# Loads, masks and the order of weight conversion in the opening of a decay-attention and softplus-FFN kernel

## The chip, the cores and the metric

One core of a Trainium2 chip. The metric is the device time of the whole program in microseconds (us). The kernel before was run three times: 659.26 us in the median, 658.81 the lowest, 661.81 the highest. One more execution was profiled.

## The reference

Linear attention with a decay per head, then a feed-forward network (FFN) with softplus:

```python
gamma = 1.0 - 2.0 ** (-5.0 - np.arange(H, dtype=np.float32))       # B, H, S, D = 4, 8, 768, 64
for t in range(S):
    state = gamma[None, :, None, None] * state + np.einsum('bhd,bhe->bhde', k[:, :, t], v[:, :, t])
    y[:, :, t] = scale * np.einsum('bhd,bhde->bhe', q[:, :, t], state)
x = y.transpose(0, 2, 1, 3).reshape(B * S, H * D)                     # 3072 tokens of 512
h = x @ w_in                                                          # 512 x 2048
g = np.maximum(h, 0.0) + np.log1p(np.exp(-np.abs(h)))
out = g @ w_out                                                       # 2048 x 512
```

All inputs reach the kernel as in the reference, the two weights as 64-bit words.

## The kernel before

**Units.** Attention runs in 48 units: a chunk of 128 tokens of one batch, and one half of the heads (four heads). A unit has loads of q, k and v (128 KB each), a decay of q and v on GpSimd (`decay`), transposes of k and q on TensorE into one PSUM bank (`tp`) with copies into `kz` (one half on ScalarE, one on VectorE) and `qs` (`operands`), scores (`sc`, `scores_whole`), a copy of the scores to SBUF on ScalarE (L268) and the causal mask on GpSimd (`mask`, L260), an update of the state (`stp`), and the product (`yp`, `outputs`), whose result is split into a high and a low part, `xh` and `xl`. There is one `kz`, written anew by each unit. Units below `WHOLE` (12) work so; later ones load blocks of 32 tokens and transpose on VectorE.

**FFN.** Four units make a pair of chunks (256 tokens). Steps are (pairs, f): `hidden` multiplies by two blocks of 128 columns of w_in, `softplus` works on VectorE, ScalarE and GpSimd, and `second`, LAG (2) steps later, multiplies by the two blocks of w_out. Steps 0 to 3 (below `TURN`) are pair 0 with f 0 to 7, steps 4 to 11 pair 1 with f 0 to 15, and from step 12 on pair 0 (f 8 to 15) goes with pair 2, and so on. Every matmul of the FFN is made of three with split operands.

**Weights.** There are 16 blocks f of w_in and of w_out, 512 KB each in 64-bit words. A block is loaded by SP and converted: for w_in one operation of ScalarE (L85), three of VectorE (L93 to L95), a cast on ScalarE (L97) and the low half on GpSimd (L98); for w_out one of the VectorE operations is on ScalarE (L91). `load_weights(f)` issues w_in f and w_out f; from f = FETCH (3) on, each waits for the conversion of block f - FETCH of its kind. `convert_weights(f)` converts w_in f and then w_out f.

**Order.** The program is written in ticks (16 for a unit; `PARTS` says at which tick a part of a unit comes), with the weights put between them, and after each step `convert_to` sets how many blocks are converted by then. A planner that estimates times turns this into an order for each engine and for the SP queue; only from step 12 on is TensorE's order the written one. Two units are loaded ahead of everything, then w_in 0 and w_out 0, then units and weights in turn. `block_decays` (written at step 4) loads a small table, `qblocks`, with 16 DMAs (L538) and extends it on GpSimd (L544); unit 12 is the first to use it. `attention_bank` gives the PSUM bank of `tp`, `sc` and `yp`, by turns `acc3` and `a`.

Of the kernel before, what the change touches and what calls it, by code (L numbers as in the profile page):

```python
# [11 lines left out]
F32R = mybir.dt.float32r  # L12
I64 = mybir.dt.int64
# [4 lines left out]
P = 128  # L18
# [5 lines left out]
EARLY = 2  # L24
# [4 lines left out]
FETCH = 3  # L29
# [4 lines left out]
def decay_attention_then_softplus_ffn(ctx: ExitStack, tc: tile.TileContext, q, k, v, w_in, w_out, qtab, vtab, gtab, out):  # L34
# [25 lines left out]
    ident = const.tile([P, P], F32, name="ident")  # L60

# [3 lines left out]
    def load_weights(f):  # L65
        fs = slice(f * P, (f + 1) * P)
        raw[f] = [const.tile([P, ND * P], I64, name=nm, tag=f"{nm}{f}") for nm in ("win", "wout")]
        loads_of_f = (
            nc.sync.dma_start(raw[f][0].rearrange("p (c w) -> p c w", c=ND), w_in[:, fs].rearrange("(c p) w -> p c w", p=P)),
            nc.sync.dma_start(raw[f][1], w_out[fs, :]),  # L70
        )

        if f >= FETCH:
            for load, after in zip(loads_of_f, converts[f - FETCH]):
                tc.add_manual_dep(load.ins, after.name, mybir.DependencyInfo(mybir.DependencyClass.Sync, mybir.DependencyReason.SCHED_ONLY), reason="pace")

    def convert_weights(f):

        n = ND * P
        converts[f] = []  # L80
        for nm, bits, to in zip(("win", "wout"), raw.pop(f), (win, wout)):
            words = bits.bitcast(U32).rearrange("p (n t) -> p n t", t=2)
            low, high = words[:, :, 0], words[:, :, 1]

            nc.scalar.activation(high.bitcast(F32), high.bitcast(F32), AF.Copy, scale=2.0**-112)  # L85

            wp = ps_o.tile([P, n], U32, name="wp", tag="acc2")
            w = ffn.tile([P, n], U32, name="w", tag="o")

            if nm == "wout":  # L90
                nc.scalar.activation(wp, low, AF.Copy, scale=(1 - SLACK) * 2.0**-29, bias=7.5 * SLACK - 0.5)  # L91
            else:
                nc.vector.tensor_scalar(wp, low, 29, None, op0=ALU.logical_shift_right)  # L93
            nc.vector.scalar_tensor_tensor(wp, high, 0x80000000, wp, op0=ALU.bitwise_and, op1=ALU.bitwise_or)
            nc.vector.scalar_tensor_tensor(w, high, 3, wp, op0=ALU.logical_shift_left, op1=ALU.bitwise_or)  # L95
            to[f] = const.tile([P, 2, n], F32R, name=f"{nm}hl", tag=f"{nm}{f}")
            converts[f].append(nc.scalar.copy(to[f][:, 0], w.bitcast(F32)).ins)  # L97
            nc.gpsimd.tensor_tensor(to[f][:, 1], w.bitcast(F32), to[f][:, 0].bitcast(F32), op=ALU.subtract)  # L98

# [22 lines left out]
    vns = [attn.tile([P, HH, 2, D], F32, name=f"vn{i}") for i in range(3)]  # L122

# [32 lines left out]
    def tokens_of(n):  # L156
        t = vns[n % 3]
# [60 lines left out]
    def attention_bank(n, shape, name):  # L218
        taken.append(n)
        if n < WHOLE and len(taken) % 2:  # L220
            return ps_o.tile(shape, F32, name=name, tag="acc3")
        return ps_a.tile(shape, F32, name=name, tag="a")
# [108 lines left out]
    def outputs(n):  # L331
# [4 lines left out]
        if n < WHOLE:  # L336
            kn, vn, a = rest
            yp = attention_bank(n, [P, NJ, C], "yp")
            v0 = vns[n % 3].rearrange("p h t d -> p (h t) d")
# [57 lines left out]
    FIRST_TICK = -24  # L397
    PERIOD = 16
# [97 lines left out]

    def convert_to(n):
        nonlocal loaded, converted
        while converted < min(NF, n):
            convert_weights(converted)  # L500
            converted += 1
            if loaded < NF:
                load_weights(loaded)
                loaded += 1


    for n in range(2):
        load_unit(n)

# [36 lines left out]
    while done < ticks_for(0):  # L546
# [5 lines left out]
        if done % (4 * TICK) == 3 * TICK and done > 0 or done < 0 and loaded == 0:  # L552
            if loaded >= FETCH:
                convert_weights(converted)
                converted += 1
            load_weights(loaded)
            loaded += 1
# [92 lines left out]
```

## Time and profile before

| what | us |
|---|---|
| median of 3 runs | 659.26 |
| lowest and highest run | 658.81, 661.81 |
| profiled execution, its own time | 661.7 |
| its span, first to last instruction | 660.0 |
| TensorE (PE) busy | 648.3 |
| VectorE (DVE) busy | 411.9 |
| ScalarE (ACT) busy | 366.7 |
| GpSimd (POOL) busy | 319.3 |

The page gives busy times over the whole span, and matmuls overlap, so a busy TensorE is not yet one at its peak. The table of windows gives the same for stretches, with the granted clock of TensorE (1.00 is 2.4 GHz, 0.50 is 1.2 GHz) and the share of the DMA engines. The timeline shows single instructions, and in brackets how long an engine stood idle before one and what ended that. SP's rows are issues, not transfers. Names left of `<-` are written, those right of it read; L12 is line 12 of the kernel.

### The profile page before, as it was taken

Reading aid. Unit: us, or ns where it says so; the run is one execution under the profiler, and the core shown is the slowest. Engines: PE = TensorE matmul, PEld = TensorE weight load, DVE = VectorE, ACT = ScalarE, POOL = GpSimd, SP = SyncE. Lnnn points to the kernel's source line nnn. Section 1 sums busy time; section 2 is a strip of 40 time slices with the busy share of each in tenths; the row PEclk is TensorE's granted clock in tenths of the full one; section 3 lists DMA queues with packets and bytes.
Section 4 is the critical chain, followed back from the end, with each engine's and each line's share of the span. In section 5 each row is a group of like instructions: output and inputs, shape, how many; then the busy total and the mean of one; then the engine's idle time right before and its main releaser. Section 6 shows DMA issues by size and latency. Waiting matters only on the chain.

```text
span 660.0 us, 11777 instructions
## 1 busy us (share of the span) xinstructions
PE 648.3 (98%) x3762; PEld 555.2 (84%) x3762; DVE 411.9 (62%) x756; ACT 366.7 (56%) x799; POOL 319.3 (48%) x330
## 2 busy tenths in 40 slices
PE   7999999999999999999999999999999999999997
PEld 6898899888888888888888888888888888888896
DVE  5777888875685576576566665676677567522221
ACT  5867876656564555556565655565565555422221
POOL 5777758564445445444543464355345543332221
PEclk9999999999999999999999999999999999999999
DMA  9898573132223241131232132131222200000000
GB/s 241 227 260 239 161 195 86 37 76 41 42 62 62 39 96 21 26 84 35 40 84 37 35 92 35 17 82 29 46 61 48 41 19 33 0 1 33 0 33 32
DMA packets 153822, 46.69 MB, mean 71 GB/s; under 512 B 140448, under 2 KB 148640, under 8 KB 153760
## 3 DMA queue, kind: packets, MB, share of 16 engines
q1 hardware_dynamic: 153312, 45.93, 29.3%
q8 instruction: 29, 0.48, 0.3%
q14 instruction: 33, 0.27, 0.1%
q10 hardware_dynamic: 448, 0.01, 0.0%
HBM read 39.60 MB, written 6.29 MB: 70 GB/s over the span
## 4 chain that ended last, share of the span: by engine, by line
PE 92%; DMA 2%; ACT 2%; POOL 1%; issue 0%; DVE 0%; SPq 0%; POOLq 0%; ACTq 0%
PE hp L436 13%; PE hp L438 13%; PE acc L471 13%; PE acc L472 13%; PE hp L437 13%; PE acc L473 13%; PE yp L355 6%; PE sc L280 3%; PE stp L307 2%; DMA win<-in_moe_w_in_dram 2%; PE yp L345 1%; PE sc L267 1%; DMA vn<-in_v_dram 1%; PE yp L342 1%; PE tp L232 0%
## 5 line engine op out<-in xcount | busy, mean ns | idle before, releaser
L453 POOL TENSOR_TENSOR gl<-sp,gh 128x512 fp32r<-128x512 f32 x96 | 129.4, 1349 | 122.5 <-ACT gh L451 118.2
L436 PE MATMUL hp<-xh,winhl 128*128 128x512 f32 (+1 forms) x448 | 166.1, 371 | 1.0 <-DVE sp L449 0.5
L438 PE MATMUL hp<-xh,winhl 128*128 128x512 f32 (+1 forms) x448 | 162.0, 362 | 0.5 <-POOL winhl L98 0.5
L437 PE MATMUL hp<-xl,winhl 128*128 128x512 f32 (+1 forms) x448 | 161.7, 361 | 0.0
L445 ACT ACTIVATE sp<-sp 128x512 f32<-128x512 f32 x96 | 60.7, 632 | 167.7 <-DVE sp L444 167.6
L471 PE MATMUL acc<-wouthl,gh 128*128 128x512 f32 x384 | 151.0, 393 | 0.0
L472 PE MATMUL acc<-wouthl,gh 128*128 128x512 f32 x384 | 150.3, 391 | 0.0
L473 PE MATMUL acc<-wouthl,gl 128*128 128x512 f32 x384 | 149.0, 390 | 0.0
L444 DVE TENSOR_SCALAR sp<-hp 128x512 uint32<-128x512 uint32 x96 | 66.3, 690 | 84.8 <-PE hp L438 62.4
L438 PEld LDWEIGHTS hp<-xh,winhl 128*128 128x128 f32 x448 | 84.5, 189 | 14.3 <-POOL winhl L98 0.9
L436 PEld LDWEIGHTS hp<-xh,winhl 128*128 128x128 f32 x448 | 84.6, 189 | 12.3 <-PE yp L345 0.7
L437 PEld LDWEIGHTS hp<-xl,winhl 128*128 128x128 f32 x448 | 84.8, 189 | 11.2
L451 ACT CAST gh<-sp 128x512 fp32r<-128x512 f32 x96 | 59.7, 621 | 52.1 <-PE acc L472 40.0
L449 DVE SCALAR_TENSOR_TENSOR sp<-hp,sp 128x512 f32<-128x512 f32 x96 | 65.2, 680 | 33.7 <-ACT sp L445 33.2
L260 POOL TENSOR_SCALAR_AFFINE_SELECT a<-a 128x512 f32<-128x512 f32 x48 | 36.6, 762 | 101.6 <-DVE a L281 97.1
L473 PEld LDWEIGHTS acc<-wouthl,gl 128*128 128x128 f32 x384 | 71.8, 188 | 15.1
L471 PEld LDWEIGHTS acc<-wouthl,gh 128*128 128x128 f32 x384 | 72.1, 188 | 12.4
L472 PEld LDWEIGHTS acc<-wouthl,gh 128*128 128x128 f32 x384 | 72.4, 189 | 12.0
L213 POOL TENSOR_TENSOR vn<-vn,vtabs 128x256 f32<-128x256 f32 x48 | 29.8, 621 | 83.6 <-DMA vn<-in_v_dram 71.8
L281 DVE TENSOR_REDUCE a<-sc 128x256 f32<-128x512 f32 x72 | 49.3, 685 | 4.3 <-PE sc L280 3.5
L292 POOL TENSOR_TENSOR al<-a,ah 128x512 fp32r<-128x512 f32 x36 | 47.9, 1331 | 3.1 <-ACT ah L291 3.1
L329 DVE TENSOR_TENSOR st<-stp,st 64x128 fp32r<-64x128 f32 x60 | 17.3, 289 | 44.8 <-ACT st L327 44.2
(94 smaller groups left out, 919.3 us busy)
## 6 DMA issues: line engine op xcount, KB each, us to landing
win<-in_moe_w_in_dram SPq DMA_DIRECT2D x16, 512.0 KB, 4.9
wout<-in_moe_w_out_dram SPq DMA_DIRECT2D x16, 512.0 KB, 4.4
vn<-in_v_dram SPq DMA_DIRECT2D x48, 128.0 KB, 2.8
out_dram<-o SPq DMA_DIRECT2D x24, 256.0 KB, 2.1
vn<-in_k_dram SPq DMA_DIRECT2D x30, 128.0 KB, 2.4
kb<-in_k_dram SPq DMA_DIRECT2D x208, 16.0 KB, 1.7
qb<-in_q_dram SPq DMA_DIRECT2D x208, 16.0 KB, 1.7
qn<-in_q_dram SPq DMA_DIRECT2D x12, 128.0 KB, 4.9
```

Of the source, the lines that this page charges most:

```text
L281: summed[n] = nc.vector.tensor_reduce(sums[n][:, 2 * j:2 * j + 2, :], sc.rearrange("p h t c -> p h c t"), axis=mybir.AxisListType.X, op=AL ...
L436: nc.tensor.matmul(to, lhsT=wt[:, 0, d, :], rhs=xh[:, d], start=d == 0, stop=False)
L437: nc.tensor.matmul(to, lhsT=wt[:, 0, d, :], rhs=xl[:, d], start=False, stop=False)
L438: nc.tensor.matmul(to, lhsT=wt[:, 1, d, :], rhs=xh[:, d], start=False, stop=d == ND - 1)
L444: nc.vector.tensor_scalar(sp.bitcast(U32), hps[s].bitcast(U32), 0x80000000, None, op0=ALU.bitwise_or)
L445: nc.scalar.activation(sp, sp, AF.Softplus)
L449: nc.vector.scalar_tensor_tensor(g, hps.pop(s), 0.0, g, op0=ALU.max, op1=ALU.add)
L451: nc.scalar.copy(gh, g)
L453: nc.gpsimd.tensor_tensor(gl, sps.pop(s), gh.bitcast(F32), op=ALU.subtract)
L471: nc.tensor.matmul(to, lhsT=gh[:, k, ts], rhs=wt[:, 0], start=first, stop=False)
L472: nc.tensor.matmul(to, lhsT=gh[:, k, ts], rhs=wt[:, 1], start=False, stop=False)
L473: nc.tensor.matmul(to, lhsT=gl[:, k, ts], rhs=wt[:, 0], start=False, stop=last)
```

## The change

The loads of weights become a list of items, w_in 0, w_in 1, then w_in f and w_out f - 2 by turns, and w_out 14 and 15. Loads and conversions go by item, loads up to six items ahead of conversions. Units 0 to 3 are loaded ahead of all weights; unit 3's v has a tile of its own, in a buffer of `sp`. A table `INITIAL` says by which tick how many items are loaded and converted. For units 0 to 3 the mask is an AND with a table of all ones or zero bits on VectorE, which reads the scores from PSUM and writes them to SBUF. `qblocks` is copied out of `qtabs` on VectorE. The turns of the two PSUM banks are swapped.

```diff
-EARLY = 2
-FETCH = 3
+FETCH = 6
...
+    items = [("win", f) for f in range(2)] + [it for f in range(2, NF) for it in (("win", f), ("wout", f - 2))]
+    items += [("wout", f) for f in range(NF - 2, NF)]
+    def load_item(i):
+        nm, f = items[i]
...
+        if i >= FETCH:
+            paced_by(load, i - FETCH)
...
+    def convert_item(i):
...
+    vns.append(ffn.tile([P, HH, 2, D], F32, name="vn3", tag="sp"))
+    def v_tile(n):
+        return vns[3 if n == 3 else n % 3]
...
-        if n < WHOLE and len(taken) % 2:
+        if n < WHOLE and len(taken) % 2 == 0:
             return ps_o.tile(shape, F32, name=name, tag="acc3")
...
-        nc.scalar.copy(a, sc)
-        mask(a)
+        if n < 4:
+            keep = causal.bitcast(U32).unsqueeze(1).broadcast_to([P, HH, C])
+            nc.vector.tensor_tensor(a.bitcast(U32), sc.bitcast(U32), keep, op=ALU.bitwise_and)
+        else:
+            nc.scalar.copy(a, sc)
+            mask(a)
...
+    INITIAL = {12: (4, 0), 28: (6, 1), 44: (6, 2), 60: (6, 4), 76: (6, 5)}
...
+    def load_to(n):
+        while loaded < min(len(items), n):
+            load_item(loaded)
+            loaded += 1
...
+        while converted < min(len(items), n):
+            convert_item(converted)
             converted += 1
+            load_to(converted + FETCH)
...
-    for n in range(2):
+    for n in range(4):
         load_unit(n)
+    load_to(2)
...
+    keep = causal.bitcast(F32)
+    nc.gpsimd.memset(keep, -1.0)
+    nc.gpsimd.affine_select(keep, keep, pattern=[[1, C]], compare_op=ALU.is_ge, fill=0.0, base=0, channel_multiplier=-1)
+    nc.vector.tensor_copy(causal, keep)
...
-        for at in range(0, P, 32):
+        for par, half, _ in sides:
+            at = half.start
             for i in range(C // 32):
-                nc.sync.dma_start(
-                    qblocks[at:at + 32, 0, :, :, i].rearrange("p f m -> p (f m)"), qtab[i * 32:(i + 1) * 32, at // D:H:2]
+                nc.vector.tensor_copy(
+                    qblocks[at:at + 32, 0, :, :, i].rearrange("p f m -> p (f m)"), qtabs[i * 32:(i + 1) * 32, 0, par:H:2]
                 )
+            nc.vector.tensor_copy(qblocks[at + 32:at + 64, 0], qblocks[at:at + 32, 0])
...
-        if done % (4 * TICK) == 3 * TICK and done > 0 or done < 0 and loaded == 0:
-            if loaded >= FETCH:
-                convert_weights(converted)
-                converted += 1
-            load_weights(loaded)
-            loaded += 1
+        if done in INITIAL:
+            load_to(INITIAL[done][0])
+            convert_to(INITIAL[done][1])
...
-        convert_to(fs[-1] + 1)
         stages(s)
-        convert_to((2 * (s + 1) if s < TURN else TURN + s + 2) + EARLY)
+        convert_to(4 * (s + 2) if s < TURN else 4 * (TURN + 1) + 2 * (s + 2 - TURN))
```

## Rows read from the trace of the kernel before

**Rows 1.** The page: engine busy times, then the span in 40 slices for TensorE (busy tenths):
```profile
PE 648.3 (98%) x3762; PEld 555.2 (84%) x3762; DVE 411.9 (62%) x756; ACT 366.7 (56%) x799; POOL 319.3 (48%) x330
...
PE   7999999999999999999999999999999999999997
```

**Rows 2.** The table of windows: stretch and its length in us, then busy us and instructions of PE, PEld, DVE, ACT and POOL, TensorE's granted clock, DMA share, GB/s:
```profile
0.00:9.40 9.40, 7.28 (x30) 6.56 (x31) 3.52 (x18) 2.87 (x5) 4.90 (x16) 1.00 0.76 194
9.40:31.60 22.20, 19.09 (x132) 16.67 (x131) 15.69 (x29) 17.71 (x38) 14.96 (x19) 0.92 0.97 259
31.60:47.80 16.20, 16.20 (x118) 15.07 (x116) 11.93 (x22) 12.31 (x26) 13.61 (x22) 1.00 0.89 236
47.80:70.00 22.20, 19.77 (x152) 18.28 (x150) 16.55 (x30) 16.69 (x34) 15.55 (x19) 1.00 0.82 238
120.00:600.00 480.00, 480.00 (x2715) 404.93 (x2714) 307.73 (x569) 266.58 (x600) 221.58 (x214) 1.00 0.22 46
```

**Rows 3.** The timeline of TensorE alone: start and duration in us, line, result and operands, what it waited for:
```profile
6.72 2.04 PE L267 MATMUL sc<-qs,kz 128*128 128x128 f32 x8
...
11.14 1.06 PE L267 MATMUL sc<-qs,kz 128*128 128x128 f32 x8
...
15.94 0.89 PE L307 MATMUL stp<-vn,kn 128*128 128x128 f32 x4 [0.77 <-POOL vn L213]
16.62 1.92 PE L267 MATMUL sc<-qs,kz 128*128 128x128 f32 x8
...
21.82 0.39 PE L436 MATMUL hp<-xh,winhl 128*128 128x256 f32 x1 [0.46 <-ACT xh L346]
22.09 1.16 PE L267 MATMUL sc<-qs,kz 128*128 128x128 f32 x8
```

**Rows 4.** The table of windows for one stretch of 3 us, columns as in the second group:
```profile
16.00:19.00 3.00, 3.00 (x16) 2.99 (x16) 2.73 (x5) 2.12 (x5) 1.75 (x2) 0.56 1.09 342
```

**Rows 5.** The timeline of all engines, columns as in the third group:
```profile
7.02 0.61 POOL L213 TENSOR_TENSOR vn<-vn,vtabs 128x256 f32<-128x256 f32 x1 [0.80 <-DMA vn<-in_v_dram]
...
8.80 0.58 ACT L268 COPY a<-sc 128x512 f32<-128x512 f32 x1 [1.26 <-PE sc L267]
...
10.14 1.16 PE L345 MATMUL yp<-a,vn 128*128 128x128 f32 x8
...
10.84 0.69 ACT L85 ACTIVATE win<-win 128x512 f32<-128x512 f32 x1
...
12.00 0.61 POOL L206 TENSOR_TENSOR qn<-qn,qtabs 128x256 f32<-128x256 f32 x1 [1.91 <-DMA qn<-in_q_dram]
...
14.05 1.27 POOL L98 TENSOR_TENSOR winhl<-w,winhl 128x512 fp32r<-128x512 f32 x1
...
31.96 0.69 DVE L444 TENSOR_SCALAR sp<-hp 128x512 uint32<-128x512 uint32 x1 [1.38 <-PE hp L438]
```

**Rows 6.** The timeline of the SP queue: time and length of the issue of each load:
```profile
4.41 0.51 SPq L69 DMA_DIRECT2D win<-in_moe_w_in_dram  x1
...
5.51 0.43 SPq L178 DMA_DIRECT2D qn<-in_q_dram  x1
...
12.19 0.42 SPq L178 DMA_DIRECT2D vn<-in_v_dram  x1
...
22.45 0.53 SPq L70 DMA_DIRECT2D wout<-in_moe_w_out_dram  x1
```

**Rows 7.** The view of DMAs from 4 to 20 us, then from 20 to 40 us: packets, the hardware queue's share, issues with the median us to landing:
```profile
DMA packets 8014, 4.70 MB, mean 294 GB/s; under 512 B 5979, under 2 KB 7630, under 8 KB 8014
...
wout<-in_moe_w_out_dram SPq DMA_DIRECT2D x3, 512.0 KB, 7.3
...
q1 hardware_dynamic: 8070, 4.08, 78.8%
```

**Rows 8.** Groups of instructions: VectorE and ScalarE from 9.4 to 47.8 us, then small ones from 0 to 130 us; count, busy us, mean ns, idle time before them:
```profile
L94 DVE SCALAR_TENSOR_TENSOR wp<-wout,wp 128x512 uint32<-128x512 uint32 x6 | 4.2, 694 | 5.5 <-ACT wp L91 5.5
...
L235 DVE COPY kz<-tp 64x256 f32<-64x256 f32 x6 | 2.6, 428 | 1.8 <-ACT kz L234 1.7
...
L91 ACT ACTIVATE wp<-wout 128x512 uint32<-128x512 uint32 x6 | 3.8, 636 | 0.0
...
L97 ACT CAST wouthl<-w 128x512 fp32r<-128x512 f32 x5 | 3.1, 621 | 0.1
...
L236 ACT COPY qs<-tp 128x256 f32<-128x256 f32 x6 | 2.2, 374 | 1.4 <-DVE kz L235 1.3
...
L532 DVE TENSOR_TENSOR vtabs<-vtabs,gtab_sb 128x8 f32<-128x8 f32 x5 | 1.1, 230 | 0.0
...
masks.py:199 POOL TENSOR_SCALAR_AFFINE_SELECT ident<-ident 128x128 f32<-128x128 f32 x1 | 0.3, 292 | 0.1
```

**Rows 9.** The chain of waits from 42 to 70 us (start, length, what); then two rows of the timeline there:
```profile
42.34 6.54 DMA win<-in_moe_w_in_dram
...
59.71 5.20 DMA win<-in_moe_w_in_dram
...
48.30 0.38 PE L438 MATMUL hp<-xh,winhl 128*128 128x256 f32 x1 [0.27 <-POOL winhl L98]
...
49.65 0.61 POOL L206 TENSOR_TENSOR qn<-qn,qtabs 128x256 f32<-128x256 f32 x1 [1.10 <-DMA qn<-in_q_dram]
```

**Rows 10.** The view of one line, L538, the table's DMAs (issue ns: least, median, most):
```profile
L538 SPq DMA_DIRECT2D qblocks<-in_qtab_dram x16: 565/594/1262, 20.8 to 37.0; - x16
```

More of the change, by code (lines that the diff above doesn't have):

```diff
@@ L12 @@
 F32R = mybir.dt.float32r
+I32 = mybir.dt.int32
 I64 = mybir.dt.int64
@@ L60, in decay_attention_then_softplus_ffn @@
     ident = const.tile([P, P], F32, name="ident")
+    causal = const.tile([P, C], I32, name="causal")
     raw, win, wout, converts = {}, {}, {}, {}
-    def load_weights(f):
+    items = [("win", f) for f in range(2)] + [it for f in range(2, NF) for it in (("win", f), ("wout", f - 2))]
+    items += [("wout", f) for f in range(NF - 2, NF)]
+    def load_item(i):
+        nm, f = items[i]
         fs = slice(f * P, (f + 1) * P)
[L67 to L75, printed above, removed]
@@ L77, in convert_weights @@
-    def convert_weights(f):
-        n = ND * P
[L80 to L98, printed above, removed]
@@ new lines, in load_item, with paced_by @@
+        raw[i] = const.tile([P, ND * P], I64, name=nm, tag=f"{nm}{f}")
+        if nm == "win":
+            load = nc.sync.dma_start(raw[i].rearrange("p (c w) -> p c w", c=ND), w_in[:, fs].rearrange("(c p) w -> p c w", p=P))
+        else:
+            load = nc.sync.dma_start(raw[i], w_out[fs, :])
+        if i >= FETCH:
+            paced_by(load, i - FETCH)
+    def paced_by(load, i):
+        tc.add_manual_dep(load.ins, converts[i].name, mybir.DependencyInfo(mybir.DependencyClass.Sync, mybir.DependencyReason.SCHED_ONLY), reason="pace")
@@ new lines, in convert_item @@
+    def convert_item(i):
+        n = ND * P
+        nm, f = items[i]
+        to = {"win": win, "wout": wout}[nm]
+        words = raw.pop(i).bitcast(U32).rearrange("p (n t) -> p n t", t=2)
+        low, high = words[:, :, 0], words[:, :, 1]
+        nc.scalar.activation(high.bitcast(F32), high.bitcast(F32), AF.Copy, scale=2.0**-112)
+        wp = ps_o.tile([P, n], U32, name="wp", tag="acc2")
+        w = ffn.tile([P, n], U32, name="w", tag="o")
+        if nm == "wout":
+            nc.scalar.activation(wp, low, AF.Copy, scale=(1 - SLACK) * 2.0**-29, bias=7.5 * SLACK - 0.5)
+        else:
+            nc.vector.tensor_scalar(wp, low, 29, None, op0=ALU.logical_shift_right)
+        nc.vector.scalar_tensor_tensor(wp, high, 0x80000000, wp, op0=ALU.bitwise_and, op1=ALU.bitwise_or)
+        nc.vector.scalar_tensor_tensor(w, high, 3, wp, op0=ALU.logical_shift_left, op1=ALU.bitwise_or)
+        to[f] = const.tile([P, 2, n], F32R, name=f"{nm}hl", tag=f"{nm}{f}")
+        converts[i] = nc.scalar.copy(to[f][:, 0], w.bitcast(F32)).ins
+        nc.gpsimd.tensor_tensor(to[f][:, 1], w.bitcast(F32), to[f][:, 0].bitcast(F32), op=ALU.subtract)
@@ L156, in tokens_of @@
     def tokens_of(n):
-        t = vns[n % 3]
+        t = v_tile(n)
         if n < WHOLE:
@@ L338, in outputs @@
             yp = attention_bank(n, [P, NJ, C], "yp")
-            v0 = vns[n % 3].rearrange("p h t d -> p (h t) d")
+            v0 = v_tile(n).rearrange("p h t d -> p (h t) d")
             for j in range(NJ):
@@ L612, in decay_attention_then_softplus_ffn @@
             block_decays()
-        convert_to(fs[-1] + 1)
+        assert {("win", f) for f in fs} <= set(items[:converted])
+        assert s < LAG or {("wout", f) for f in steps[s - LAG][1]} <= set(items[:converted])
         stages(s)
-        convert_to((2 * (s + 1) if s < TURN else TURN + s + 2) + EARLY)
+        convert_to(4 * (s + 2) if s < TURN else 4 * (TURN + 1) + 2 * (s + 2 - TURN))
     with tc.manual_schedule(engines={mybir.EngineType.PE}):
```

9 lines of the change are left out of this document (3 added, 6 removed).

## The prediction

> **What bounds the kernel now.** I read the page's engine times and slices first: the reader sees TensorE busy for 648.3 of 660.0 us, and its slices below 9 only at the start and the end [rows 1]. So a gain can only come from places where TensorE waits, works at the low clock, or has nothing to do. The table of windows says where these are [rows 2]. From 120 to 600 us no idle time is left. Up to 9.4 us TensorE is idle for 2.12 us, from 9.4 to 31.6 us for 3.11 us, from 31.6 to 47.8 us for nothing, from 47.8 to 70 us for 2.43 us: 7.7 us, 1.2% of the time.
>
> The matmuls in order of time then show a loss that busy time hides [rows 3]. A unit's eight score matmuls take 2.04 us at 6.72 and 1.92 us at 16.62, but 1.06 us at 11.14. From 16 to 19 us the granted clock is 0.56 in the mean, so mostly the lower of its two levels, behind a wait of 0.77 us [rows 3, 4]. The units 0 to 3 follow each other slowly: scores start at 6.72, 11.14, 16.62 and 22.09 us, so 4.4, 5.5 and 5.5 us apart. The first FFN step needs all four; it begins at 21.82, and VectorE gets its result at 31.96 [rows 3, 5].
>
> Why are the units late? The SP queue and the waits tell [rows 5, 6]. Units 0 and 1 are issued first, then w_in 0 at 4.41 and w_out 0, then unit 2 from 5.51, then another 1 MB, then unit 3, whose last load goes at 12.19. GpSimd waits 1.91 us for unit 2's q and starts on it at 12.00, 6.5 us after its issue. The transfers move 294 GB/s from 4 to 20 us, and a w_out takes 7.3 us to land [rows 7]. The DMA engines are the bound of this stretch, so what is issued first decides. Beside it ScalarE is busy for 17.71 of 22.2 us with weight conversions between the copies of the units [rows 2].
>
> **The change part by part.** *Four units first.* The twelve loads hold 1.57 MB. Units 0 and 1 are in at 7.02 (the decay of unit 1's v starts then, having waited for it [rows 5]); at 294 GB/s a unit (0.39 MB) is 1.34 us, so units 2 and 3 land near 8.4 and 9.7, where unit 2's q is there at 12.0 today and unit 3's last load is not even issued before 12.19. No load gates the four units any more. What then spaces them is one chain: kz on ScalarE 0.37 (half a tile, as qs), kz on VectorE 0.43, qs on ScalarE 0.37, scores 1.06 at the high clock or 2.04 at the low [rows 3, 8], and four hand-overs of an estimated 0.1 (the copy of the scores at 8.80 starts 0.04 after they end at 8.76): 2.6 or 3.6 us. Bounds of the spacing: 2.6, and 4.4, which units 0 and 1 have today, whose loads were both early. I take 3.6, nearest to the rows of this stretch, where two of three scores run at the low clock. Three spacings make 10.8 instead of 15.4 us, so unit 3's scores come 4.6 us sooner; with 2.6 it is 7.6, with 4.4 it is 2.2.
>
> *The mask.* Today the scores' copy starts at 8.80 on ScalarE, GpSimd selects, and the product starts at 10.14: 1.34 us [rows 5]. After: one VectorE operation from PSUM of the same size, nearest row 0.69 (L94 [rows 8]), plus a hand-over: 0.75. The operation with a broadcast mask has no row: 0.69 to 1.4 (twice the row). For units 0 to 2 the 0.6 us lies mostly beside the chain above, for unit 3 on the path: 0.6, at worst -0.1. Together the end of the first FFN step moves forward by 5.2 us (2.1 to 8.2).
>
> *Weights behind the units.* w_in 0 and 1 land 1.78 us apart at 294 GB/s, near 11.5 and 13.3, and conversion of w_in 0 begins at 11.5 instead of 10.84. It takes 4.5 us today (10.84 to the end of GpSimd's part, 14.05 and 1.27 [rows 5]), so w_in 1 is ready near 18, ahead of unit 3. That costs nothing, covered by the units' chain; without the cover it costs 0.7 us.
>
> *w_out two items later.* Up to TURN a step needs two new w_in, and their w_out only LAG steps later. So w_in 7 becomes the 13th load instead of the 15th: 2 x 1.78 = 3.6 us of transfer, and ahead of it 2 x 1.39 us less of VectorE (two operations) and 2 x 1.95 us less of ScalarE (0.69, 0.64 and 0.62) [rows 5, 8]. It gates today: TensorE waits at 48.30 for GpSimd's half of a w_in [rows 9].
>
> *Decay table.* Sixteen DMAs of 0.5 KB leave SP; the median issue is 0.594 us, 9.5 us in all, from 20.8 on, with weight issues queued among them [rows 6, 10]. From 20 to 40 us the hardware queue's share is 78.8% [rows 7], so some 4 us of transfer time are left unused there. Ten small VectorE copies come instead: nearest row 0.23 (128x8 [rows 8]), so 1.2 (half of it) to 2.3 us, I take 1.9; not on TensorE's path as long as VectorE has room, and wanted only for unit 12.
>
> *Small additions.* The mask's memset and select on GpSimd, 0.29 each by the select for ident [rows 8], may stand ahead of the decay of unit 0's q: 0 to 0.6, I take 0.2, as others of its memsets can go behind. A memset and a copy on VectorE lie beside the first loads. The swapped banks and the fourth v tile in sp's second buffer cost nothing: step 0 has the first buffer, and unit 3 is done before step 1 wants the second; without that, 0.7 us of VectorE's pass.
>
> **What remains of 5.2 us.** From 31.6 to 47.8 us TensorE has no idle time today, so the advance is kept there until w_in 7. TensorE comes to it near 42.6 instead of 47.8. The load is 3.6 us sooner by order and up to 4 more by the SP queue; the conversion is bound by VectorE. That is busy 27.6 of 38.4 us from 9.4 to 47.8 [rows 2]; it gains 2.8 (masks) and 1.9 (copies) and loses 2.8: 29.5 us. At today's 72% this takes 41 us, at 85% 34.7. Its largest wait is for ScalarE's wp, 5.5 us [rows 8], and ScalarE loses 2.3 us of copies and 3.9 of conversions, so I take 82%: 36 us from 9.9 on, so w_in 7 near 46, 3.4 us behind TensorE. Work on unit 7, whose q [rows 9] comes some 4 us sooner with the same stream, covers half of it: loss 1.7. The idle 2.43 us of 47.8 to 70 us hang on two w_in transfers of 6.54 and 5.20 us for which ScalarE stands still, with the copies of a unit behind [rows 9]; I count 0.9 as won (-1 to 2.4).
>
> Sum: 5.2 - 0.2 - 1.7 + 0.9 = 4.2 us. The profiled execution took 661.7 us (span 660.0), 2.4 us above the median of 659.26; on its own time the sum gives 657.5, on the median 655.0, which I forecast.
>
> **Rivals.**
> *The weights give it back (same).* If VectorE stays nearer 77%, w_in 7 is ready at 48 as now, and the advance is waited off but for the unit that fills: 1 to 2.5 us remain, 657.5. For it: masks and copies go to the engine that converts. Against: 5.5 us of its idle time is a wait for ScalarE.
>
> *VectorE becomes the gate (slower).* If it stays at 72%, w_in 7 comes at 50.9, 3.1 us later than today. If unit 7's q is again not there (GpSimd waits 1.10 us for it until 49.65 today [rows 9]), nothing fills the time, and it is 659.3 + 3.1 = 662.4. The point from which it decides: 29.5 us of work from 9.9 on must end by 47.8, so below 78% this takes the whole advance and more.
>
> *The clock stays low (same).* The units of 9 to 20 us are short bursts with waits between. If the clock is low there as long as between the scores of units 0 and 1, the spacing is 4.4 instead of 3.6, and 2.4 us of the gain go: 657.4. The Trainium skill, "TensorE: Matmul & The Clock Gate", section "HAM oscillation", says that waits for DMA between short bursts of matmuls make the clock fall back, so that each burst starts at half rate. The trace agrees with that rule in the row from 16 to 19 us, 0.56 granted.
>
> *All stalls go (faster).* Spacing 2.6 and no wait for w_in 7 give at most 8.2 + 2.4 - 0.2 = 10.4 us; with the spacing alone, 651.
>
> **How the numbers follow.** Forecast, 653 to 657: 0.54. Weights give it back: 0.18; clock stays low: 0.06; VectorE the gate: 0.12; all stalls go: 0.10. About 0.5% (3.3 us) is what a measurement of this kernel tells from no change, so faster means under 656.0: the faster rival and 0.50 of the forecast's 0.54, 0.60; same 0.28, the rest of the forecast and the two rivals near 657.5; slower 0.12. The range from 650.8 to 660.5 leaves out the upper part of the gate rival and the far end of the fastest.
>
> **What would show it.** Right: scores of units 0 to 3 some 3.6 us apart and unit 3's near 17.7; no wait for q of units 2 and 3; the first FFN result near 26.8; no small DMAs from 20 to 38 us and a fuller DMA share there. Wrong: scores still over 4.4 us apart (chain or clock); TensorE waiting over 3 us for w_in halves from 40 to 50 us with VectorE under 78% busy; ScalarE held by w_in transfers with copies of units behind.

## The result and the profile after

The changed kernel takes 664.51 us in the median of five runs (662.94 to 666.41), the kernel before 659.76 us in five runs (658.81 to 661.81). The ratio is 1.0073, with a 95% interval of 1.0045 to 1.0100: slower, where 655.0 and faster had been forecast, and outside the range. The profiled execution took 665.68 us, of which 663.7 are its span.

The page of the kernel after: busy times, and of the 40 slices the row of TensorE and that of its clock.

```profile
PE 650.5 (98%) x3762; PEld 555.9 (84%) x3762; DVE 416.7 (63%) x772; ACT 364.0 (55%) x795; POOL 317.4 (48%) x328
...
PE   8999999799999999999999999999999999999997
...
PEclk9999999799999999999999999999999999999999
```

The reader is to see a 7 in both rows, in the eighth slice (116 to 133 us), where TensorE's busy row of before had a 9 [rows 1]. The table of windows of the kernel after, columns as in [rows 2], says the same in numbers:

```profile
9.40:31.60 22.20, 20.70 (x150) 18.11 (x148) 17.10 (x32) 13.97 (x32) 12.25 (x16) 1.00 0.97 287
31.60:47.80 16.20, 15.66 (x118) 14.53 (x119) 12.54 (x23) 13.89 (x29) 13.32 (x16) 1.00 0.81 226
47.80:70.00 22.20, 21.15 (x163) 19.81 (x162) 16.80 (x30) 17.84 (x37) 15.24 (x17) 1.00 0.74 213
112.00:120.00 8.00, 7.59 (x42) 6.44 (x42) 7.12 (x15) 6.18 (x15) 3.10 (x3) 1.00 0.13 26
120.00:130.00 10.00, 6.67 (x27) 5.05 (x26) 4.58 (x8) 4.33 (x9) 6.97 (x8) 0.69 0.18 32
```

The opening is better: 18 matmuls more in the stretch from 9.4 to 31.6 us, at a granted clock of 1.00 instead of 0.92, and 11 more from 47.8 to 70 [rows 2]. But from 120 to 130 us TensorE is busy for 6.67 of 10 us at a clock of 0.69; the same window of the kernel before:

```profile
120.00:130.00 10.00, 10.00 (x57) 8.36 (x56) 7.81 (x16) 5.94 (x13) 4.84 (x5) 1.00 0.25 45
```

**How far ahead TensorE was.** The timeline of TensorE in the kernel after, columns as in [rows 3], gives the scores of units 0 to 3, the first and second scores of unit 12 and the first of unit 13:

```profile
7.38 2.08 PE L277 MATMUL sc<-qs,kz 128*128 128x128 f32 x8 [0.32 <-ACT qs L246]
...
12.51 1.06 PE L277 MATMUL sc<-qs,kz 128*128 128x128 f32 x8
...
15.35 1.06 PE L277 MATMUL sc<-qs,kz 128*128 128x128 f32 x8
...
18.65 1.16 PE L277 MATMUL sc<-qs,kz 128*128 128x128 f32 x8
...
111.71 0.40 PE L295 MATMUL sc<-kq 128*128 128x256 f32 x2
...
114.74 0.50 PE L295 MATMUL sc<-kq 128*128 128x256 f32 x2
...
130.22 0.56 PE L295 MATMUL sc<-kq 128*128 128x256 f32 x2
```

The same place in the kernel before:

```profile
115.47 0.40 PE L280 MATMUL sc<-kq 128*128 128x256 f32 x2
...
116.32 0.39 PE L438 MATMUL hp<-xh,winhl 128*128 128x256 f32 x1 [0.21 <-POOL winhl L98]
...
117.62 0.40 PE L280 MATMUL sc<-kq 128*128 128x256 f32 x2
...
122.89 0.39 PE L473 MATMUL acc<-wouthl,gl 128*128 128x512 f32 x1
123.11 0.64 PE L355 MATMUL yp<-ah,vhl 128*64 128x128 f32 x8
123.59 0.40 PE L355 MATMUL yp<-al,vhl 128*64 128x128 f32 x4
...
126.64 0.40 PE L280 MATMUL sc<-kq 128*128 128x256 f32 x2
```

Unit 3 is 3.4 us sooner than before [rows 3]. Unit 12's first scores are 3.8 us sooner, but they do not stand at the same place: three matmuls of step 12 (0.7 us) are ahead of them before and behind them after. At its second scores both kernels have done the same matmuls, and from there on their order is the same, so that is the mark to compare: the lead is 2.9 us (114.74 against 117.62). From the first scores of unit 13 to the end of the kernel TensorE is 3.6 to 3.7 us behind the kernel before. All of this, 6.5 us, is lost between the two marks:

```profile
113.44 0.38 PE L455 MATMUL hp<-xh,winhl 128*128 128x256 f32 x1 [0.41 <-POOL winhl L104]
...
120.10 0.39 PE L490 MATMUL acc<-wouthl,gl 128*128 128x512 f32 x1
122.24 0.69 PE L370 MATMUL yp<-ah,vhl 128*64 128x128 f32 x8 [1.75 <-ACT ah L306]
124.51 0.69 PE L370 MATMUL yp<-al,vhl 128*64 128x128 f32 x4 [1.57 <-POOL al L307]
125.00 0.73 PE L453 MATMUL hp<-xh,winhl 128*128 128x512 f32 x1
125.53 0.63 PE L454 MATMUL hp<-xl,winhl 128*128 128x512 f32 x1
125.96 0.63 PE L455 MATMUL hp<-xh,winhl 128*128 128x512 f32 x1
```

The wait of 0.41 us for a half of w_in 15 lies ahead of the first mark (the kernel before waits 0.21 us there). Behind the mark come the waits for the two parts of unit 12's masked scores (`ah`, `al`), 1.75 and 1.57 us; from start to start of the matmuls they cost 1.9 and 1.8 us more than the same places before. Behind them the matmuls start 0.43 us apart, up to 130.2 us, where 0.23 is the spacing at the full clock (that of the last ones before the waits): with the first two gaps, 0.2 and 0.3 us too long, and eleven of 0.20, that is 2.7 us. So 6.4 of the 6.5 us are named. The executions differ the same way: the one without any loss of clock (granted 1.000) has a span of 660.9 us, two with 0.994 have 663.7 and 664.5.

**Who was late.** The timeline of GpSimd in the kernel after, at unit 12 (L104 is the low half of a weight, L270 the mask, L307 `al`):

```profile
114.87 1.29 POOL L104 TENSOR_TENSOR wouthl<-w,wouthl 128x512 fp32r<-128x512 f32 x1 [1.48 <-ACT wouthl L103]
119.48 1.34 POOL L104 TENSOR_TENSOR wouthl<-w,wouthl 128x512 fp32r<-128x512 f32 x1 [3.33 <-ACT wouthl L103]
120.77 0.63 POOL L270 TENSOR_SCALAR_AFFINE_SELECT a<-a 128x512 f32<-128x512 f32 x1
121.38 0.61 POOL L220 TENSOR_TENSOR qb<-qb,qblocks 128x256 f32<-128x256 f32 x1
121.95 1.28 POOL L470 TENSOR_TENSOR gl<-sp,gh 128x512 fp32r<-128x512 f32 x1
123.19 1.27 POOL L307 TENSOR_TENSOR al<-a,ah 128x512 fp32r<-128x512 f32 x1
124.41 1.27 POOL L104 TENSOR_TENSOR wouthl<-w,wouthl 128x512 fp32r<-128x512 f32 x1
```

The mask starts where a conversion of w_out ends, and the last conversion comes after `al`. VectorE is as full (7.12 of 8 us from 112 to 120): it adds unit 12's second scores at 118.54, 3.8 us after TensorE has begun them (114.74), with operations of w_out at 115.37 and 117.60 ahead of that. From unit 12's second scores to the end of `al` 9.7 us pass (to 124.46), in the kernel before 5.1 (to 122.70); TensorE has 6.0 us of other matmuls to do in that time, so 5.1 is in time and 9.7 is not. The 32nd and last conversion ends at 125.7 us, in the kernel before at 117.5.

The stream was late from the start. SP, ScalarE and GpSimd in the opening of the kernel after, one timeline each:

```profile
10.51 1.26 SPq L77 DMA_DIRECT2D wout<-in_moe_w_out_dram  x1
...
22.03 0.45 SPq L75 DMA_DIRECT2D win<-in_moe_w_in_dram  x1
```

```profile
15.55 0.37 ACT L361 CAST xh<-yp 128x256 fp32r<-128x256 f32 x1 [0.38 <-PE yp L360]
15.81 0.67 ACT L91 ACTIVATE win<-win 128x512 f32<-128x512 f32 x1
```

```profile
11.97 0.61 POOL L223 TENSOR_TENSOR vn<-vn,vtabs 128x256 f32<-128x256 f32 x1
20.02 1.29 POOL L104 TENSOR_TENSOR winhl<-w,winhl 128x512 fp32r<-128x512 f32 x1 [7.44 <-ACT winhl L103]
```

w_in 0 is issued behind twelve loads of units and lands at 12.71 us (9.87 before). Its first ScalarE operation stands behind copies of units 1 and 2 and starts at 15.81, the last step starts at 20.02 instead of 14.05 [rows 5]. So the first conversion ends 6.0 us later than before (21.3 against 15.3). The stream makes up some of this: its 30th conversion ends 4.1 us later (116.2 against 112.1). The last two, which meet unit 12, end 4.5 and 8.2 us later. No weight is issued from 10.51 to 22.03, where the seventh went at 16.77 before, but that gap did not hold the stream: the cast that the seventh load has to wait for ended at 19.94, SP then still had loads of units to issue, and when the block landed at 27.52, ScalarE began on it 2.6 us later.

### The profile page after: what moved, and what is told of

Same layout as the page of the kernel before. It is cut to its first block, busy times and chain, and to the rows that moved or that the text cites. A ratio compares the mean times of both kernels' runs of the same rounds, so it can differ in the third digit from the quotient of the medians.

```text
span 663.7 us, 11761 instructions
## 1 busy us (share of the span) xinstructions
PE 650.5 (98%) x3762; PEld 555.9 (84%) x3762; DVE 416.7 (63%) x772; ACT 364.0 (55%) x795; POOL 317.4 (48%) x328
## 4 chain that ended last, share of the span: by engine, by line
PE 81%; POOL 1%; DVE 1%; ACT 1%; issue 1%; DMA 1%; SPq 0%; ACTq 0%; POOLq 0%
PE hp L453 12%; PE acc L488 12%; PE acc L489 12%; PE hp L455 12%; PE acc L490 12%; PE hp L454 12%; PE yp L370 6%; PE sc L295 2%; PE stp L322 2%; DMA wout<-in_moe_w_out_dram 1%; SPq L161 0%; DVE sp L466 0%; DVE w L101 0%; POOL gl L470 0%; POOL winhl L104 0%
## 5 line engine op out<-in xcount | busy, mean ns | idle before, releaser
L270 POOL TENSOR_SCALAR_AFFINE_SELECT a<-a 128x512 f32<-128x512 f32 x44 | 34.5, 783 | 102.1 <-DVE a L296 97.4
L307 POOL TENSOR_TENSOR al<-a,ah 128x512 fp32r<-128x512 f32 x36 | 47.8, 1326 | 2.7 <-ACT ah L306 2.7
```

## The experiments

My theory: the conversion stream starts 5 to 6 us late behind four units and, its engines having little room, is still late at unit 12, while TensorE is early; there the two meet. Rivals: the order of w_in and w_out; the work added on VectorE; the swapped banks; and a TensorE that is too early at a chain that the stream does not set. The depth of the loads (six items) and the fourth v tile were not undone by themselves. "First" and "lead" below are how much sooner than in the kernel before unit 12's first and second scores start, "kept" the same for the last score matmul of the kernel. The expectations speak of the first scores; the text behind them compares at the second, where all but the two runs with another order of items (pairs in turn, catch up) have done the same matmuls. Leads are from the one profiled execution of each run, which can be 2 us or more from the median: in "mask" (665.50) and "tail behind unit 12" (663.36) it was the slowest of ten. The runs were made in four groups, each beside runs of the kernel before (medians of 660.71 to 661.41 us; 659.76 beside the change), so differences between groups go by the ratios, times 660 us.

| run | median us | ratio, 95% interval | first | lead | kept | last conversion ends |
|---|---|---|---|---|---|---|
| the change | 664.51 | 1.0073, 1.0045 to 1.0100 | 3.8 | 2.9 | -3.7 | 125.7 |
| pairs in turn | 665.76 | 1.0081, 1.0061 to 1.0100 | 0.5 | 0.0 | -2.2 | 124.2 |
| catch up | 668.79 | 1.0127, 1.0101 to 1.0153 | 4.5 | 1.8 | -6.5 | 127.6 |
| asked sooner from step 4 | 665.21 | 1.0075, 1.0055 to 1.0096 | 4.1 | 3.0 | -1.8 | 125.2 |
| banks | 662.34 | 1.0028, 1.0015 to 1.0041 | 4.4 | 3.7 | 0.8 | 127.4 |
| mask | 662.88 | 1.0030, 1.0017 to 1.0043 | 0.6 | 0.4 | -3.8 | 129.2 |
| table | 668.70 | 1.0103, 1.0080 to 1.0125 | -1.6 | -2.0 | -7.1 | 130.3 |
| two units ahead | 660.29 | 0.9981, 0.9970 to 0.9992 | 0.6 | 1.0 | 0.9 | 117.2 |
| three w_out left out | 659.13 | 0.9970, 0.9958 to 0.9983 | 3.7 | 2.5 | 2.6 | 113.7 |
| asked sooner in the opening | 664.61 | 1.0055, 1.0037 to 1.0073 | 3.7 | 2.5 | -2.9 | 126.1 |
| w_in 0, 1 between | 660.67 | 0.9996, 0.9979 to 1.0013 | 5.5 | 5.1 | 0.6 | 124.8 |
| two units, banks | 660.35 | 0.9990, 0.9973 to 1.0006 | 1.2 | 2.0 | 2.0 | 116.2 |
| two units, banks, mask | 659.73 | 0.9987, 0.9970 to 1.0004 | 1.9 | 2.3 | 2.3 | 115.9 |
| tail behind unit 12 | 661.20 | 0.9998, 0.9981 to 1.0014 | 0.8 | 0.1 | -1.4 | 129.8 |
| between, and tail behind | 658.63 | 0.9956, 0.9941 to 0.9970 | 5.9 | 5.3 | 3.3 | 125.0 |
| between, banks | 662.78 | 1.0018, 1.0002 to 1.0034 | 3.7 | 2.0 | -1.5 | 127.4 |
| between, banks, tail behind | 663.46 | 1.0026, 1.0006 to 1.0045 | 5.3 | 5.8 | -0.6 | 127.4 |

**The order of the items.** Pairs in turn:

```diff
-    items = [("win", f) for f in range(2)] + [it for f in range(2, NF) for it in (("win", f), ("wout", f - 2))]
-    items += [("wout", f) for f in range(NF - 2, NF)]
+    items = [it for f in range(NF) for it in (("win", f), ("wout", f))]
```

> Of the changed kernel, only the item order is undone: w_in f and w_out f in turn as before, with the loads, the mask and the table as changed. Theory S (three late w_out conversions share VectorE and GpSimd with unit 12's first chain, and TensorE, whose order is fixed there, waits): w_out 13 to 15 are converted two items sooner, the two waits for ah and al at unit 12's product (1.75 and 1.57 us in the changed kernel) shrink to under 0.5 us together, the clock stays high behind them; the lead at unit 12's first scores falls from 3.8 to 1 to 3 us, since w_in 7 is the 15th load again; time 657 to 660. Theory D (TensorE only comes too early at a chain that loads and the SP queue bound): the waits stay over 2 us; 662 to 665.

The lead at unit 12 falls to nothing, so the new order is worth some 3 us of lead up to there, and the time is no better without it. The waits for `ah` and `al` are gone, as the theory had it, but the time it gave (657 to 660) is missed by far: TensorE waits 1.23 us for a half of w_in at 117.23 and 0.85 us for the softplus at 126.01 in their place. The lag only of the first blocks:

```diff
-    items = [("win", f) for f in range(2)] + [it for f in range(2, NF) for it in (("win", f), ("wout", f - 2))]
-    items += [("wout", f) for f in range(NF - 2, NF)]
+    items = [("win", f) for f in range(2)] + [it for f in range(2, 8) for it in (("win", f), ("wout", f - 2))]
+    items += [("wout", 6), ("wout", 7)] + [it for f in range(8, NF) for it in (("win", f), ("wout", f))]
```

> The changed kernel, but w_out is two items late only up to block 7; w_out 6 and 7 then come together, and from block 8 on w_in f and w_out f go in turn. Theory S: the opening is that of the changed kernel (lead at unit 12's first scores 3 to 4 us), and the last conversions end some 4 us sooner against unit 12's chain, so the waits there fall under 0.7 us together: 655.5 to 658. Theory D: the lead is there and is lost at unit 12 all the same: 661 to 665. Rival B (the swapped banks): as D.

Slower still: w_in halves are waited for now (four waits of about a microsecond from 111 to 125 us, and 2.26 us for the softplus behind them), and the stream ends at 127.6. Which weight is late changes with the order; that one is late does not.

**Asking sooner.** From step 4 on, and in the opening:

```diff
-        convert_to(4 * (s + 2) if s < TURN else 4 * (TURN + 1) + 2 * (s + 2 - TURN))
+        convert_to(4 * (s + 2) if s < TURN else 4 * (TURN + 1) + 2 * (s + 2 - TURN) + 4)
```

> The changed kernel, item order and all, but from step 4 on the program asks for four more items converted by each step. Theory S: the last w_out are converted some 5 us sooner or more, waits at unit 12 under 0.7 us, 655.5 to 659, if the conversions don't push pair 1's own work. Theory D and rival B: waits at unit 12 stay over 2 us, 661 to 665.

```diff
-    INITIAL = {12: (4, 0), 28: (6, 1), 44: (6, 2), 60: (6, 4), 76: (6, 5)}
+    INITIAL = {12: (4, 1), 28: (6, 2), 44: (6, 4), 60: (6, 5)}
```

> Four units ahead as in the changed kernel, but the table of the opening asks for conversions 16 ticks sooner (1, 2, 4 and 5 items at ticks 12, 28, 44 and 60). If it is where the conversions stand in the order of the opening that makes the stream late (ScalarE and GpSimd stand still for 4 and 8 us while w_in 0 is there from 12.7), the first conversion ends near 17 instead of 21, the last near 121, and the time falls by 2 to 4 us, to 661. If it is the loads behind four units (w_in 0 lands at 12.7 instead of 9.9), the last conversion stays over 123 and the time within 1.5 us of 664.5.

Neither moves the stream: the first conversion ends at 21 and 22 us, the last at 125.2 and 126.1, and the 655.5 to 659 that the theory gave for the first of the two are missed. I take it that the planner orders by its own estimate of when inputs are there; no run shows that.

**The banks, the mask, the table.**

```diff
-        if n < WHOLE and len(taken) % 2 == 0:
+        if n < WHOLE and len(taken) % 2:
```

> The changed kernel with the turns of the two PSUM banks as before. Rival B: the waits at unit 12 go, 656 to 659. Theory S: they stay over 2 us together, and the time stays at 661 to 666.

```diff
-        if n < 4:
+        if n < 0:
```

> Masks of units 0 to 3 back on ScalarE and GpSimd, the rest as in the changed kernel. Added VectorE work is what makes the conversions late: four masks of 0.69 us leave VectorE, the last conversion ends some 3 us sooner than 125.7 and the time falls by 2 to 3 us, to 662. The late start behind four units is the cause: VectorE gets 2.8 us back but the stream still starts 6 us late, last conversion over 124 us, time within 1.5 us of 664.5. TensorE too early at a chain that the stream does not set: unit 3 loses some 0.6 us of its lead, time unchanged or 0.5 us longer.

```diff
-                nc.vector.tensor_copy(
-                    qblocks[at:at + 32, 0, :, :, i].rearrange("p f m -> p (f m)"), qtabs[i * 32:(i + 1) * 32, 0, par:H:2]
+                nc.sync.dma_start(
+                    qblocks[at:at + 32, 0, :, :, i].rearrange("p f m -> p (f m)"), qtab[i * 32:(i + 1) * 32, at // D:H:2]
                 )
-            nc.vector.tensor_copy(qblocks[at + 32:at + 64, 0], qblocks[at:at + 32, 0])
```

> The decay table loaded by 16 DMAs again, the rest as in the changed kernel. Added VectorE work is the cause: ten copies go from VectorE, unit 0's scores come 0.7 us sooner, 1 to 2 us faster than the changed kernel. Late start of the stream: SP gets 9.5 us of issues back into the stretch of 20 to 40 us, in which the late conversions wait for loads, so the last conversion ends 0 to 3 us later and the time is the same or up to 3 us longer.

Banks and mask take 3.0 and 2.8 us off by the ratios. With the old banks both waits for `ah` and `al` are gone (one of 1.89 us for the softplus is there instead) although the stream ends even later (127.4): the waits as the rival had them, the time as the theory had it. I read this as a price of the banks, which the later runs refuted. With the mask back the waits at unit 12 are 1.08 and 0.95 us and the stream ends 3.5 us later, not sooner: added VectorE work is not what makes it late. Where the 2.8 us come from stays open. The table is the other way: with its DMAs again the kernel is 2.0 us slower by the ratios, whose intervals overlap, and its lead at unit 12 goes from 2.9 to -2.0 us. The timeline of SP in that run shows what is behind it:

```profile
21.46 2.62 SPq L567 DMA_DIRECT2D qblocks<-in_qtab_dram  x4
24.19 0.52 SPq L188 DMA_DIRECT2D vn<-in_v_dram  x1
24.75 0.57 SPq L567 DMA_DIRECT2D qblocks<-in_qtab_dram  x1
25.42 0.54 SPq L75 DMA_DIRECT2D win<-in_moe_w_in_dram  x1
```

The seventh weight is issued at 25.42 instead of 22.03, with five of the small DMAs ahead of it, and here ScalarE does stand idle for the loads (2.64 us until the ninth weight is there at 36.09).

**The stream itself.** Two units ahead of the weights instead of four, and three conversions left out:

```diff
-    for n in range(4):
+    for n in range(2):
         load_unit(n)
```

> Two units ahead of the weights instead of four, the order of items, the mask and the table as in the changed kernel. Late start of the stream is the cause: the first conversions end some 3 to 5 us sooner (first near 17 instead of 21 us), the last near 120, the waits of 1.75 and 1.57 us at unit 12 shrink, and the time falls by 2 to 4 us, though units 2 and 3 come 1 to 3 us later. If the ticks of conversion and not the loads hold the stream, its last end stays at 125 and the time is 664 or more. Added VectorE work as the cause: no change, 664.5.

```diff
+    items = [it for it in items if it not in (("wout", 13), ("wout", 14), ("wout", 15))]
...
+    wout[13] = wout[14] = wout[15] = wout[12]
     with tc.manual_schedule(engines={mybir.EngineType.PE}):
```

> Leaves out the load and conversion of w_out blocks 13, 14 and 15 and multiplies by w_out 12 in their place, so part of the second product uses other weights; the matmuls and all else are as in the changed kernel. The tail of the stream is the cause: with three items fewer the last conversion ends 6 us or more sooner, near 119, no wait over 1 us is left at unit 12, no fall of the clock at 125 us, and the time is 657 to 660, about the forecast of 655 and below the kernel before. TensorE too early at a chain that the stream does not set: the waits at unit 12 stay, 663 to 665.

Both agree with the theory. With two units the first low half starts at 14.79 us and the last conversion ends at 117.2, nothing is lost from unit 12 on, and the kernel is 6.1 us faster than the change, a little faster than the one before. TensorE is only 1.0 us early there, so this run does not tell a stream in time from a TensorE that has little to lose; the next does. With three items fewer, and the opening untouched, `ah` and `al` are there when TensorE comes, as its timeline in that run shows:

```profile
120.58 0.64 PE L371 MATMUL yp<-ah,vhl 128*64 128x128 f32 x8
121.05 0.40 PE L371 MATMUL yp<-al,vhl 128*64 128x128 f32 x4
```

From unit 12's second scores to the end of `al` 4.9 us pass (115.08 to 120.01). By the ratios the tail of the stream was worth 6.8 us. That the chain of unit 12 is late by itself is refuted.

**Where w_in 0 is loaded.**

```diff
-    for n in range(4):
+    for n in range(2):
         load_unit(n)
     load_to(2)
+    for n in range(2, 4):
+        load_unit(n)
```

> Loads of w_in 0 and w_in 1 between units 1 and 2, units 2 and 3 ahead of all other weights. If the late landing of w_in 0 is the cause, it lands near 10 again and the last conversion ends near 119, time 660 to 661. If it is where the conversions are asked for (tick 28), the first still ends near 20, and the time stays within 1.5 us of 664.5; units 2 and 3 lose some 3 us of their lead in either case.

w_in 0 lands at 9.56 us and the first conversion ends at 16; 660.67, as expected. Not as expected, the stream still ends at 124.8, while TensorE is 5.1 us early at unit 12; 4.4 of these are lost there, with waits of 1.32 and 0.96 us for `ah` and `al`. So the late start is not the whole cause. Here the first conversion is in time, the 30th ends at 113.9 us (112.1 before), and it is the last two, w_out 14 and 15, that fall behind, at 119.9 and 124.8 (the last two before ended at 116.3 and 117.5): TensorE is at unit 12 by 112.57, ahead of them, and its chain and theirs share the engines. The other combinations:

> Two units ahead of the weights and the turns of the two PSUM banks as before, the rest as in the changed kernel. If the two add (4.2 us for two units, 2.2 us for the banks, against 664.5), 658 us, 0.3 to 0.5% below the kernel before. If the banks only mattered because the stream was late at unit 12, no more than two units alone give: 660.3.

> As the run with two units and the banks as before, and the masks of units 0 to 3 back on ScalarE and GpSimd: what is left of the change is the order of the items, the depth of the loads and the copied table. If VectorE is what bounds the conversions once they start in time, 2.8 us less of it is worth 1 to 2 us over the run with the mask on VectorE. If the mask's own step of 0.6 us counts, units 1 to 3 come later and it is 0.5 to 1 us slower than that run.

0.9990 and 0.9987 against 0.9981: with two units ahead neither the banks nor the mask makes a difference that these runs can tell. With w_in 0 and 1 between the units and the next edit, the old banks cost 4.8 us (658.63 and 663.46, below, in one group). So the banks have no one price, and what I read from the first of these runs falls; that they act by shifting the planner's order is my reading and not shown. The other way round it bounds what the loads are worth: with the old banks, two units ahead bring 2.5 us (1.0028 to 0.9990) and w_in 0 and 1 between the units 0.7 us (1.0028 to 1.0018), where the swapped ones gave 6.1 and 5.1. Each edit makes the planner order the whole anew, and some microseconds of each difference can be that.

**Order or amount?** What was open is whether the last conversions cost because they stand ahead of unit 12 in the queues, or because the engines lack time whatever stands first. The first two of these runs move only the order (names as in the kernel); the other two set it against the old banks, without and with the edit:

```diff
-        nc.scalar.activation(high.bitcast(F32), high.bitcast(F32), AF.Copy, scale=2.0**-112)
+        first = nc.scalar.activation(high.bitcast(F32), high.bitcast(F32), AF.Copy, scale=2.0**-112)
+        if i >= len(items) - 2:
+            behind(first, masked[12], "unit 12 first")
...
-        convert_to(4 * (s + 2) if s < TURN else 4 * (TURN + 1) + 2 * (s + 2 - TURN))
+        convert_to(4 * (s + 2) if s < TURN else min(len(items) - 2, 4 * (TURN + 1) + 2 * (s + 2 - TURN)))
...
             paced_stages(s)
+            convert_to(len(items))
```

> The changed kernel with one edit: the conversions of the last two items (w_out 14 and 15) are planned behind the mask of unit 12 instead of ahead of it; amount of work, loads and opening are the same. If what costs at unit 12 is that the tail of the stream stands in the queues of VectorE, ScalarE and GpSimd ahead of the chain of unit 12, the waits of 1.75 and 1.57 us and the half clock behind them go, and the time falls by 4 to 5 us, to about 660. If the engines are short of time whatever stands first, w_out 14 and 15 are waited for a step later, and the time stays over 663.

> The run with w_in 0 and 1 loaded between units 1 and 2, with the last two conversions behind the mask of unit 12 as well. That run had a lead of 5.5 us over the kernel before at unit 12 and kept 0.6 of it. If the queue order at unit 12 takes it, 3 to 4 us of the lead stay and the time is 656 to 658; if the total work of the converters does, 660 to 661.

> The run with w_in 0 and 1 between units 1 and 2, with the turns of the two PSUM banks as before. If the banks delay the opening by themselves (unit 1's scores 1.4 us sooner with the old turns), the lead at unit 12 grows to 6 us or more, and as the wait there takes it, the time stays at 660 to 661. If the banks matter at unit 12 itself, 658.

> All three edits: w_in 0 and 1 between units 1 and 2, old turns of the banks, the last two conversions behind the mask of unit 12. By the theory of the late stream whose tail stands ahead of unit 12: 655 to 657, below the kernel before by 0.6% or more. By the rival that the converters' total work sets the time of unit 12: 660.

The timeline of GpSimd in the first of them (L272 is the mask, L309 `al`, L106 the low half) shows the new order, and that of TensorE in the second what is left:

```profile
120.82 0.81 POOL L272 TENSOR_SCALAR_AFFINE_SELECT a<-a 128x512 f32<-128x512 f32 x1 [2.52 <-DVE a L298]
121.60 0.61 POOL L222 TENSOR_TENSOR qb<-qb,qblocks 128x256 f32<-128x256 f32 x1
122.73 1.29 POOL L309 TENSOR_TENSOR al<-a,ah 128x512 fp32r<-128x512 f32 x1 [0.51 <-ACT ah L308]
123.98 1.29 POOL L472 TENSOR_TENSOR gl<-sp,gh 128x512 fp32r<-128x512 f32 x1
125.26 1.30 POOL L106 TENSOR_TENSOR wouthl<-w,wouthl 128x512 fp32r<-128x512 f32 x1
```

```profile
119.37 0.45 PE L372 MATMUL yp<-al,vhl 128*64 128x128 f32 x4 [0.66 <-POOL al L309]
...
125.08 0.50 PE L491 MATMUL acc<-wouthl,gh 128*128 128x512 f32 x1 [0.61 <-POOL wouthl L106]
```

The one edit takes 5.0 us off the change, and from unit 12 on 1.6 us are lost instead of 6.6; the clock stays at its full level there. It is not a clean pair, since the planner also moved earlier work (a wait of 1.99 us at 68 us), and with 0.1 us of lead left at unit 12 there is little to lose. The second pair is cleaner, with leads of 5.1 and 5.3 us: 4.4 us are lost without the edit and 2.0 with it, and the ratio goes from 0.9996 to 0.9956, 2.6 us. What is left are waits for `al` and for w_out 15, whose low half ends at 125.0, so there the amount begins to count. With the old banks the edit brings nothing (1.0018 and 1.0026), and neither run ends where either theory had it: in the first the lead does not grow but falls to 2.0 us, in the second unit 12 passes with 4.9 us of lead, and the next step waits 1.35 and 1.27 us for halves of the last w_out, with the clock at 0.79 from 125 to 130 us. So both theories hold in part: the order decides what waits first, the unfinished stream that something must wait. When the stream ends does not by itself tell the time: the runs "banks", "mask" and "tail behind unit 12" end it later than the change and are faster. 658.63 is the fastest version that converts all weights, 0.44% (0.30 to 0.59%) below the kernel before.

## Why the prediction was wrong

**What bounds the kernel.** "From 120 to 600 us no idle time is left" was right of the kernel before, and I took it for a stretch in which nothing can be lost. There the kernel before was just in time: its last conversion ended at 117.5 us, and TensorE had waited 0.21 us for the half of w_in 15 at 116.32. The loss lies from 120 to 130 us.

**Four units first.** Right in sum, in part by luck: spacings of 5.1, 2.8 and 3.3 us where 3.6 each was forecast, the first outside the bounds of 2.6 to 4.4 and the other two below the value taken; together 11.3 against 10.8. Unit 0's scores took 2.08 us, twice unit 1's 1.06, although the profile grants 1.00 there; why stays open. Unit 3 was 3.4 us sooner instead of 4.6, of which 0.7 us is unit 0's own delay (below). The first FFN result came at 26.47 us, forecast near 26.8. The clock from 16 to 19 us was 1.00 where [rows 4] had 0.56, so the rival of the low clock fell.

**Small additions and the table.** Unit 0 was 0.7 us later, forecast 0.2: the planner put the ten copies, costed as wanted only for unit 12, ahead of unit 0's `kz`, which starts on VectorE at 6.50 instead of 5.80. With the DMAs again unit 0's scores start at 6.75. The table itself may be a gain of some 2 us in the changed kernel (the intervals overlap), by way of the weights whose issue the DMAs hold up; the sum had the copied table only as cover for w_in 7.

**The step that failed: "Weights behind the units ... costs nothing, covered by the units' chain".** I forecast the start of w_in 0's conversion at 11.5 and w_in 1 ready near 18; its GpSimd half started at 20.02, and w_in 1 was ready at 23.9. The landing was 1.2 us off, but ScalarE took the conversion 3.1 us after it, behind the copies of the units, and the conversions behind followed late. The cover was real for TensorE in the opening, not for the stream, which was still 4.1 us late at its 30th conversion. In the changed kernel two units ahead instead of four are worth 6.1 us, w_in 0 and 1 between the units 5.1; with the old banks 2.5 and 0.7. So the step failed, but how much of the loss is its own, and how much the planner's order, these runs do not settle.

**Where the sum ended.** It came to 4.2 us, and the lead at unit 12 was 2.9. But I closed the account at w_in 7, and the stream goes on for 19 more conversions, to unit 12, where the lead and 3.7 us more were lost: the masked scores waited behind the conversion of w_out 14, and the clock fell. Without the last three conversions the changed kernel is 6.8 us faster. Every rival had its price at w_in 7 and none there, so the range could not hold it. "VectorE becomes the gate" had the kind of loss right, by the wrong cause: not VectorE's added work (the run with the old mask) but a stream not yet done at unit 12 and the order of the queues.

**w_in 7.** The wait at 48.30 us [rows 9] was for w_in 5, the sixth low half of a w_in, ended at 48.2; I had taken the load in flight for the block that was waited for. The half of w_in 7 ended at 61.2 before and at 58.6 after, and TensorE waited for it in neither. The forecast loss of 1.7 us did not come.

**Banks at nothing.** Not true of the change as it was made: with the old banks 3.0 of the 4.8 us by which it is slower are back. Nor is it a price that holds: nothing with two units, 4.8 us the other way in the fastest kernel. What stays open is why; I found no number in the profile that tells it ahead of a run.

## What to carry to other kernels

When work is moved ahead of a stream of loads and conversions, follow the stream to its last item and set its end against the advance: both can come to the same place, and a lead that the stream cannot follow is lost there, with the clock on top. Compare two kernels at a mark ahead of which both have done the same work; a first instruction of a kind can have moved among its neighbours. A stretch without idle time in the profile of before says that everything was in time, not that it has room. Where the stream's tail meets a chain that TensorE wants first, look at what stands first in each engine's queue; moving two conversions behind one mask was worth 2.6 us in the cleaner of two pairs, with no work less, and nothing with the old banks. Where a planner orders the rest, repeat an edit beside another one before its price is believed.

## What the runs showed of the hardware

Two waits of 1.75 and 1.57 us, 2.3 us apart and with little work between them, were followed by some 5 us at the lower clock (0.50 in a window from 125 to 130 us): 2.7 us on top of 3.3 us of waiting. Waits of 0.46 or 0.66 us in their place left the clock at its full level, and so did waits of 1.08 and 0.95 us (the run "mask") and a single one of 1.89 us ("banks"). After 1.74 and 1.57 us ("asked sooner in the opening") it was 0.66 from 125 to 130 us, after 1.32 and 0.96 us ("w_in 0, 1 between") 0.69 from 120 to 125 us, so like waits do not cost the same in each run. The Trainium skill, "TensorE: Matmul & The Clock Gate", section "HAM oscillation", says that waits for DMA between short bursts of matmuls make the clock fall back, so that the next burst starts at half rate. The trace agrees on the fall, but here the waits were for ScalarE and GpSimd and not for a DMA; ahead of the row at 0.56 [rows 4], too, the wait of 0.77 us was for GpSimd [rows 3].
